# The first chunk of a fused attention and expert kernel: scores in other banks, another order of its first products, transposes done later, casts of v on another engine

## The chip, the cores and the metric

The kernel runs on one core of a Trainium2 chip. The metric is the device time of one execution in microseconds (us). The engines are named as the profile names them: PE (TensorE, the matmuls; PEld is its loading of weights), ACT (ScalarE), DVE (VectorE), POOL (GpSimd) and SP (SyncE, which issues nearly all DMAs here). Each has its own list of instructions in the program and waits for the others on semaphores.

## What is computed

For each of 8 batches, with 2496 tokens, 256 columns of v and u and 64 of z, attention without a softmax; then a choice of one of 8 experts for each token, of which an expert takes 80 at most, the ones with the largest gate.

```
scores = (z @ z.T) / S                  # z: 2496 x 64
attn   = maximum(scores, 0) ** 2
x      = u * (attn @ v)                 # v, u: 2496 x 256

expert  = argmax(x @ w_gate)            # 8 experts
for each expert e: its 80 tokens of largest gate weight
    out[token] = gate * (relu(x[token] @ w1[e]) @ w2[e])
```

Scores are symmetric in queries and keys. The kernel uses it: a block of scores is computed once, and its mirror image is gained by a transpose.

## The kernel before

Tokens are padded to 20 tiles of 128; four tiles are a chunk of queries (512 columns), so a batch (b) has five chunks (qc). Keys are taken in pairs of tiles (k, k + 1), ten pairs to a chunk; four tiles of keys are a block (j). One turn of the main loop (L1144) is a step (b, qc, r): it makes the scores of the pair that is two steps ahead (LOOK = 2) and the products of the pair of this step.

**A pair on its way.** `scores` (L396) lets PE multiply z with z, three products in a high part (zh) and a low part (zl): high by high, low by high, high by low, each for two tiles of keys that lie on the two halves of PE's rows and run together. The result s takes two PSUM banks. The pool `ps_s` has one such buffer, so PE can start a pair's scores only when ACT's Relu (L415) has emptied the buffer of the pair before. ACT then squares in place (L417), giving a, and casts it to its high part ah (L115); DVE subtracts to the low part al (L58, from L440). The casts of the first two pairs are on DVE (L117). The products (`weigh`, L452) go into acc: high v by ah, low v by ah, high v by al (the table THREE, L465); each of these, for one tile and one half of the 256 output columns, is again two matmuls that run together.

**Values.** A block of v comes by DMA into vraw, is cast to its high half (`prep_vh`, on ACT for blocks 1 to 3 of the first chunk, L1176) and its low half is subtracted on DVE (`prep_vl`, L148). Both are called vt in the rows.

**Mirrors.** In the first chunk of a batch all keys are scored. For blocks j above the chunk's own, a is also transposed on DVE (`mirror`, L312, L317), two pairs to a block, written to DRAM in a layout that completes the transpose (y, L327, two steps later), and read back (blk, L344) into one of four buffers a0 to a3 for the later chunk whose queries are block j. There `mirrored` (L377) casts and subtracts it in the place of scores. A block (i, j) in these words is the one that chunk i reads for keys of block j. A list `free` holds the buffers that no block has; a read waits until one is free, its write was issued two steps before, and its use is at most 12 steps away.

**Order.** The engines' orders are written by hand (`manual_schedule`, L1133): what stands in the code is the order on each engine. Before the loop, seven matmuls on zeros (`warm(7)`), the z blocks 0 and 1, v block 0, the scores of the first two pairs, and eight more matmuls on zeros (`warm(WARM0, True)`, L1139) in the two banks of pool `ps_m`. These matmuls on zeros are called fillers below.

Of the kernel before, what the change touches and what calls it, by code (L numbers as in the profile page):

```python
# [8 lines left out]
F32 = mybir.dt.float32  # L9
# [10 lines left out]
P = 128  # L20
# [5 lines left out]
def attn_moe_kernel(ctx, tc, zT, uT, v, wg, w1, w2, out, seq, cap):  # L26
# [114 lines left out]
    def prep_vh(b, g, raw, e0):  # L141
        vt = vpool.tile([P, QT, 2, D], F32R, tag="vt", name=f"vt_{b}_{g}")
        cp(e0, vt[:, :, 0], raw)
        v_t[b, g] = vt
# [19 lines left out]
    idle = const.tile([P, CH], BF16, name="idle")  # L164
    nc.gpsimd.memset(idle, 0.0)

    def warm(n, halves=False):
        wm = ps_m.tile([P, 2, CH], F32, tag="m", name=f"warm_{nid()}")
        for i in range(n):
            if not halves:  # L170
                nc.tensor.matmul(wm[:, 0], idle[:, :P], idle, start=True, stop=True)
                continue
            for h, hs in enumerate(HALVES):
                nc.tensor.matmul(wm[:, h], idle[hs, :P], idle[hs], start=True, stop=True)

    warm(7)
    vraw0 = load_v(0, 0)
# [124 lines left out]

    half_t, y_t, blk, slot_of, free = {}, {}, {}, {}, list(range(NA))
    n32 = P // SQ
    now, to_write = [0], []

# [65 lines left out]
    def pair_tile(tag, b, qc, k, dt=F32R, bufs=3):  # L374
        return ew.tile([P, 2, CH], dt, tag=tag, name=f"{tag}_{b}_{qc}_{k}", bufs=bufs)
# [17 lines left out]

    turned = []

    def scores(b, qc, k, turn=False):  # L396

        if k // QT < qc:
            if turn and qc % 2 == 0:
                return None, lambda: (mirrored(b, qc, k, 0), mirrored(b, qc, k, 1))  # L400
            return None, lambda: mirrored(b, qc, k)
        nq = min(CH, seq - qc * CH)
        diag = k // QT == qc and not whole_block(b, qc)
        lower = diag and k % QT > 0
        c0, c1 = (HQ, nq) if lower else (0, CH if diag else nq)
        a = pair_tile("a", b, qc, k, F32, 2)
        s = ps_s.tile([P, 2, CH], F32, tag="s", name=f"s_{b}_{qc}_{k}")
        kh, kl = (z[b, k // QT] for z in (zh_t, zl_t))
        qh, ql = (z[b, qc][:, c0:c1] for z in (zh_t, zl_t))
        for n, (zk, zq) in enumerate(((kh, qh), (kl, qh), (kh, ql))):  # L410
            for h, hs in enumerate(HALVES):
                t = k % QT + h
                nc.tensor.matmul(s[:, h, c0:c1], zk[hs, t * P:(t + 1) * P], zq[hs],  # L413
                                 start=n == 0, stop=n == 2)
        nc.scalar.activation(out=a[:, :, c0:c1], in_=s[:, :, c0:c1], func=AF.Relu)  # L415
        def square():
            nc.scalar.activation(out=a[:, :, c0:c1], in_=a[:, :, c0:c1], func=AF.Square)  # L417

        def cast():
            split(b, qc, k, a, diag, lower, c0, nq)  # L420

        if turn:
            return square, cast
        square()
        return None, cast

    def split(b, qc, k, a, diag, lower, c0, nq):
        ah = pair_tile("ah", b, qc, k)
        al = pair_tile("al", b, qc, k)
        if lower:  # L430
            m = quarter.pop((b, qc))[1].rearrange("p n k (t s) -> p k t n s", t=2)

            def natural(o):
                return o[:, :, :HQ].rearrange("p k (t n s) -> p k t n s", t=2, s=SQ)

            nc.scalar.copy(out=natural(ah), in_=m)
            tt(natural(al), m, natural(ah), ALU.subtract)
        on_v = k // QT == qc and qc == 0 or (qc, k) in ON_V and b > 0
        cp(V if on_v else nc.scalar, ah[:, :, c0:nq], a[:, :, c0:nq])
        tt(al[:, :, c0:nq], a[:, :, c0:nq], ah[:, :, c0:nq], ALU.subtract)  # L440
        if diag and not lower:
            if qc:
                quarter_out(b, qc, a)
            else:
                turned.append(lambda: quarter_out(b, qc, a))
        if k // QT > qc:
            mirror(b, k // QT, qc, k % QT, a)
        a_t[b, qc, k] = (ah, al)

# [28 lines left out]
    def attend_end(b, qc, final=()):  # L478

        k = NT - 1  # L480
        weigh(b, qc, k, 0, 0, 0, 0, False)
        weigh(b, qc, k, 0, 1, 0, 1, 0 in final)
        weigh(b, qc, k, 0, 0, 1, 0, 0 in final)
        weigh(b, qc, k, 1, 1, 1, 0, False)
        weigh(b, qc, k, 1, 0, 0, 1, 1 in final)
        weigh(b, qc, k, 1, 1, 0, 0, 1 in final)

    def attend_pair(b, qc, k, by_half=False, final=False, between=None):

# [546 lines left out]

    RAW = {(qz, 4): (2, 1)}
    WARM = 4, 3
    WARM0 = 4
    keys_in = {qc: [(qc - 1, 1, 6)] for qc in range(1, NQ)}  # L1040
    keys_in[0] = []
    keys_in[NQ - 1] = [(NQ - 2, 1, 4), (NQ - 1, 4, 7)]
# [90 lines left out]
    with tc.manual_schedule(engines={ET.PE, ET.Activation, ET.DVE, ET.SP, ET.Pool}):  # L1133
# [2 lines left out]
        prep_z(0, 1, raw12[:, 0])  # L1136
        for k in (0, 2):
            scores(0, 0, k)[1]()
        warm(WARM0, True)  # L1139
        v_raw[0, 1] = vraw1  # L1140
        z_raw.update({(0, 2): raw12[:, 1], (0, 3): raw34[:, 0], (0, 4): raw34[:, 1]})
        constants()
# [1 line left out]
        for i, (b, qc, r) in enumerate(steps):  # L1144
            last = b == B - 1 and qc == NQ - 1
            now[0] = i
            if (b, qc) == (0, 0) and r in (0, 2, 4):
                prep_z(0, r // 2 + 2, z_raw.pop((0, r // 2 + 2)))
            if i + LOOK < len(steps):
                nb, nqc, nr = steps[i + LOOK]  # L1150
                square, cast = scores(nb, nqc, 2 * pairs_of[nb, nqc][nr], r == NP - 1)
            p = pairs_of[b, qc][r]
            if r == NP - 1 and not last:
                def between(c):
                    take(b, qc, c)
                    if c == 0:
                        if square:
                            square()
                        while turned:
                            turned.pop()()  # L1160

                attend_pair(b, qc, 2 * p, True, True, between)
            if i + LOOK < len(steps):
                cast()
            shift = 1 if qc == 0 else 0
            if r == shift and prev:
                chunk_add(*prev)
            if r == 1 + shift and prev:
                chunk_x(*prev)
            if b == 0 and qc == 0:  # L1170
                if r == 5:
                    prep_vh(0, NQ - 1, v_raw[0, NQ - 1], V)
                if r % 2 == 0 and r < 8:
                    g = r // 2 + 1
                    if g < NQ - 1:
                        prep_vh(0, g, v_raw[0, g], nc.scalar)  # L1176
                    prep_vl(0, g, v_raw.pop((0, g)), V)
                    if g + 1 < NQ:
                        v_raw[0, g + 1] = load_v(0, g + 1)
                if r == 8:  # L1180
                    constants_v()
            if (b, qc, r) == (0, 2, 8):
                row_constants()
            if last and r >= NP - 2:
                if r == NP - 2:
                    for c in range(DC):
                        attend(b, qc, 2 * p, c)
            elif r < NP - 1:
                attend_pair(b, qc, 2 * p, r == 0)
            if prev:  # L1190
                finished(*prev, r)

            nb, nqc = (b, qc + 1) if qc + 1 < NQ else (b + 1, 0)
            if r == 4:
                prep_u(b, qc)
            if b + 1 < B:
                for j, load, prep in keys_in[qc]:
                    if r == prep:
                        prep_z(b + 1, j, z_raw.pop((b + 1, j)))
                    if r == load:  # L1200
                        z_raw[b + 1, j] = load_z(b + 1, j)
                if (qc, r) in V_LOAD:
                    g = V_LOAD.index((qc, r))
                    v_raw[b + 1, g] = load_v(b + 1, g)
                if (qc, r) in V_HIGH:
                    g = V_HIGH.index((qc, r))
                    prep_vh(b + 1, g, v_raw[b + 1, g], V if g == NQ - 1 else nc.scalar)
            v_low(b, qc, r)
            if qc == 0 and 0 < b < B - 1 and r < ZEROS and (b - 1) * ZEROS + r < B * NQ:
                zero_out((b - 1) * ZEROS + r, B * NQ)  # L1210
            if 2 <= b < B - 1 and qc < 2 and r in TURN:
                turn(TURN.index(r))
            if b == B - 1 and qc >= NQ - 3:
                weights_ahead(qc, r)
            if (b, qc, r) in two_at:
                two_at[b, qc, r]()
            if b == B - 1 and (qc, r) in x_at:
                x_at[qc, r]()
            mirror_back()
            mirror_out()  # L1220
            quarter_write()
            if r == 3 and not whole_block(b, qc):
                quarter_back(b, qc)
            if r == NP - 1:
                prev = b, qc
# [486 lines left out]
```

## Time and profile before

| | us |
|---|---|
| median of three runs | 1310.31 (1308.8, 1310.31, 1313.16) |
| the profiled execution, its own time | 1307.35 |
| its span, from the first to the last instruction | 1305.6 |
| PE busy in it | 1289.4 (99%) |
| DVE busy | 1062.5 (81%) |
| ACT busy | 1011.9 (78%) |

The first chunk of the first batch, with which the change deals most, lasts until about 43 us of the span. A row of the timeline has the start, the duration (of the whole group, where several instructions are merged, xN), the engine, the source line, the operation, output and inputs by their names, the shape, and in brackets the idle time of that engine before it with what ended it. Windows give the busy time of an engine in a stretch and, in brackets, how many of its instructions began there.

### The profile page before, as it was taken

The numbers are of one execution on the slowest core, as the hardware profiler recorded it, in microseconds if no ns is written. First come the engines' busy times: TensorE is split into PE (matmuls) and PEld (weight loads), VectorE is DVE, ScalarE is ACT, GpSimd is POOL, SyncE is SP. The second block draws the span as 40 slices with busy tenths as digits, with TensorE's granted clock in tenths as the row PEclk, the third lists the DMA queues.
The fourth block names the chain that finished last, engine by engine and source line by source line (L and its number), as shares of the span: only waits on it lengthen the run. The fifth ranks groups of instructions, "written<-read, shape, count | busy, mean of one in ns | idle before, by whom it ended". The sixth has DMA issues, their size and how long they took to land. (4 is left out here: it accounts for less than half of the span.)

```text
span 1305.6 us, 31273 instructions
## 1 busy us (share of the span) xinstructions
PE 1289.4 (99%) x13109; PEld 1069.3 (82%) x13109; DVE 1062.5 (81%) x1281; ACT 1011.9 (78%) x1120; POOL 53.9 (4%) x66
## 2 busy tenths in 40 slices
PE   9999999999999999999999999999999999999996
PEld 6887888888888888888888888888888888887886
DVE  8878788778886888887987788877887878877785
ACT  8877688777878678776887778876787868877785
POOL 0000000000000000001000040000000000003022
PEclk9999999999999999999999999999999999999998
DMA  6678768895989959998699967999699984789853
GB/s 209 229 233 241 218 225 261 231 267 186 277 270 261 264 202 301 262 261 257 218 308 271 283 216 231 278 265 278 221 271 257 258 254 122 237 255 257 258 189 136
DMA packets 196132, 317.21 MB, mean 243 GB/s; under 512 B 36192, under 2 KB 119056, under 8 KB 185744
## 3 DMA queue, kind: packets, MB, share of 16 engines
q1 hardware_dynamic: 194704, 312.85, 80.2%
q0 software_dynamic: 1280, 2.30, 0.6%
q8 instruction: 104, 1.70, 0.5%
q14 instruction: 44, 0.36, 0.1%
HBM read 168.77 MB, written 141.21 MB: 237 GB/s over the span
## 5 line engine op out<-in xcount | busy, mean ns | idle before, releaser
L461 PE MATMUL acc<-ah,vt 64*128 64x512 f32 (+1 forms) x6240 | 954.0, 383 | 0.7 <-ACT xf L534 0.4
L461 PEld LDWEIGHTS acc<-ah,vt 64*128 64x128 f32 x6240 | 584.7, 184 | 117.6 <-ACT xf L534 8.7
L461 PE MATMUL acc<-al,vt 64*128 64x512 f32 (+1 forms) x3120 | 610.3, 382 | 1.8 <-DVE al L58 1.5
L58 DVE TENSOR_TENSOR al<-a,ah 128x1024 fp32r<-128x1024 f32 (+1 forms) x240 | 270.7, 1128 | 139.9 <-ACT ah L115 137.5
L461 PEld LDWEIGHTS acc<-al,vt 64*128 64x128 f32 x3120 | 299.8, 184 | 59.0 <-DVE al L58 4.5
L415 ACT ACTIVATE a<-s 128x1024 f32<-128x1024 f32 x240 | 229.1, 955 | 140.4 <-PE s L413 120.1
L417 ACT ACTIVATE a<-a 128x1024 f32<-128x1024 f32 x240 | 238.1, 992 | 7.4
L58 DVE TENSOR_TENSOR al<-blk,ah 128x1024 fp32r<-128x1024 f32 (+1 forms) x176 | 194.2, 1121 | 44.9 <-ACT ah L391 44.9
L391 ACT CAST ah<-blk 128x1024 fp32r<-128x1024 f32 (+1 forms) x176 | 165.0, 973 | 74.2 <-PE acc L461 63.0
L115 ACT CAST ah<-a 128x1024 fp32r<-128x1024 f32 (+3 forms) x217 | 213.6, 984 | 5.7
L317 DVE STREAM_TRANSPOSE x<-a 128x1024 f32<-128x1024 f32 x160 | 198.1, 1238 | 0.0
L58 DVE TENSOR_TENSOR xf<-xf 128x1024 f32<-128x1024 f32 (+2 forms) x110 | 137.2, 1247 | 0.0
L413 PE MATMUL s<-zh,zl 64*128 64x512 f32 x480 | 89.7, 370 | 0.0
L413 PE MATMUL s<-zl,zh 64*128 64x512 f32 x480 | 89.6, 370 | 0.0
L534 ACT COPY xf<-acc 128x1024 f32<-128x1024 f32 x64 | 64.9, 1016 | 24.1 <-PE acc L461 24.1
L413 PE MATMUL s<-zh,zh 64*128 64x512 f32 x320 | 63.4, 393 | 0.2 <-ACT a L415 0.2
L413 PEld LDWEIGHTS s<-zl,zh 64*128 64x128 f32 x480 | 45.1, 185 | 8.2
L413 PEld LDWEIGHTS s<-zh,zl 64*128 64x128 f32 x480 | 45.2, 185 | 7.1
L148 DVE TENSOR_TENSOR vt<-vraw,vt 128x1024 fp32r<-128x1024 f32 x40 | 48.1, 1202 | 0.0
L549 DVE SCALAR_TENSOR_TENSOR xf<-xf,ut 128x1024 f32<-128x1024 f32 (+1 forms) x39 | 45.8, 1174 | 0.0
L413 PEld LDWEIGHTS s<-zh,zh 64*128 64x128 f32 x320 | 30.0, 184 | 6.6 <-ACT a L415 0.7
L634 PEld LDWEIGHTS <-xf 64*128 64x128 bf16 x1872 | 26.1, 93 | 9.9 <-issue 9.9
(203 smaller groups left out, 672.4 us busy)
## 6 DMA issues: line engine op xcount, KB each, us to landing
y<-x SPq DMA_DIRECT2D x80, 1024.0 KB
blk<-y SPq DMA_DIRECT2D x320, 256.0 KB
out<-idle SPq DMA_DIRECT2D x40, 512.0 KB
vraw<-v SPq DMA_DIRECT2D x32, 512.0 KB
ut<-uT SPq DMA_DIRECT2D x32, 512.0 KB
xu<-xf SPq DMA_DIRECT2D x32, 512.0 KB
wraw<-w SPq DMA_DIRECT2D x30, 512.0 KB
yd<-xd SPq DMA_DIRECT2D x37, 256.0 KB
```

The lines of the kernel that those rows point to most:

```text
L58: V.tensor_tensor(out=o, in0=a, in1=b, op=op)
L115: eng.copy(out=o, in_=i)
L148: e1.tensor_tensor(out=vt[:, :, 1], in0=raw, in1=vt[:, :, 0], op=ALU.subtract)
L317: V.transpose(out=x[:, :, :, t:t + 2].rearrange("p n k t s -> p t k n s"), in_=a)
L391: nc.scalar.copy(out=natural(ah), in_=src[:, rows])
L413: nc.tensor.matmul(s[:, h, c0:c1], zk[hs, t * P:(t + 1) * P], zq[hs], start=n == 0, stop=n == 2)
L415: nc.scalar.activation(out=a[:, :, c0:c1], in_=s[:, :, c0:c1], func=AF.Relu)
L417: nc.scalar.activation(out=a[:, :, c0:c1], in_=a[:, :, c0:c1], func=AF.Square)
L461: nc.tensor.matmul(acc_t[b, qc][c][:, h, :nq], v_t[b, k // QT][hs, k % QT, iv, c * P:(c + 1) * P], x[hs, k % 2, :nq], start=at not in begu ...
L534: nc.scalar.copy(out=x[:, :, c], in_=acc)
L549: V.scalar_tensor_tensor(out=x[:, 0], in0=x[:, 0], scalar=CSQ, in1=u_t[b, qc][:, :, :x.shape[-1]], op0=ALU.mult, op1=ALU.mult)
L634: nc.tensor.matmul(to[:, h, t], xb[i % 3][hs, i // 3, t0:t0 + P], wgs[hs, i // 3], start=i == 0, stop=i == 3 * DC - 1)
```

## The change

- **Banks.** The scores of the third pair of the first chunk (k = 4) go to the two banks of `ps_m` instead of `ps_s`.
- **Fillers.** The eight matmuls on zeros before the loop are left out.
- **Order of products.** In step 0 the products that need ah alone, of both tiles, come first, and those that need al after them (`attend_first`).
- **Transposes.** In the first chunk the squared scores of blocks 2, 3 and 4 are written not to the two turning buffers of a but to the buffers a1, a2 and a3, which hold them. Their six transposes are done later: both of block 2 after step 0 of chunk 1, those of block 3 after steps (1, 7) and (2, 2), those of block 4 after (2, 2) and (2, 7). The list of free buffers begins with a0 alone; a1 to a3 join when their block is transposed.
- **Casts.** The casts of v's blocks 1, 2 and 3 in the first chunk are on DVE instead of ACT.

```diff
-    def warm(n, halves=False):
+    def warm(n):
         wm = ps_m.tile([P, 2, CH], F32, tag="m", name=f"warm_{nid()}")
         for i in range(n):
-            if not halves:
-                nc.tensor.matmul(wm[:, 0], idle[:, :P], idle, start=True, stop=True)
-                continue
-            for h, hs in enumerate(HALVES):
-                nc.tensor.matmul(wm[:, h], idle[hs, :P], idle[hs], start=True, stop=True)
+            nc.tensor.matmul(wm[:, 0], idle[:, :P], idle, start=True, stop=True)
...
-    half_t, y_t, blk, slot_of, free = {}, {}, {}, {}, list(range(NA))
+    half_t, y_t, blk, slot_of, free = {}, {}, {}, {}, [0]
+    held = {}
...
+    def weights_tile(b, qc, k):
+
+        j = k // QT
+        if (b, qc) != (0, 0) or j < 2:
+            return pair_tile("a", b, qc, k, F32, 2)
+        if k % QT == 0:
+            held[j] = apool.tile([P, 2, 2, CH], F32, tag=f"a{j - 1}", name=f"a_held_{j}")
+        return held[j][:, k % QT // 2]
+
+    def mirror_held(j, t):
+        mirror(0, j, 0, t, held[j][:, t // 2])
+        if t:
+            free.append(j - 1)
+
+    held_at = {(1, 0): [(2, 0), (2, 2)], (1, 7): [(3, 0)], (2, 2): [(3, 2), (4, 0)], (2, 7): [(4, 2)]}
...
-        a = pair_tile("a", b, qc, k, F32, 2)
-        s = ps_s.tile([P, 2, CH], F32, tag="s", name=f"s_{b}_{qc}_{k}")
+        a = weights_tile(b, qc, k)
+        pool, tag = (ps_m, "m") if (b, qc, k) == (0, 0, 4) else (ps_s, "s")
+        s = pool.tile([P, 2, CH], F32, tag=tag, name=f"s_{b}_{qc}_{k}")
...
-        if k // QT > qc:
+        if k // QT > qc and ((b, qc) != (0, 0) or k // QT < 2):
             mirror(b, k // QT, qc, k % QT, a)
...
+    UPPER, LOWER = THREE[:2], THREE[2:]
+
+    def attend_first(tiles, products):
+
+        for iv, al in products:
+            for t in tiles:
+                for c in range(DC):
+                    for h in range(2):
+                        weigh(0, 0, t, c, h, iv, al, False)
...
-        warm(WARM0, True)
...
                     if g < NQ - 1:
-                        prep_vh(0, g, v_raw[0, g], nc.scalar)
+                        prep_vh(0, g, v_raw[0, g], V)
...
+            elif i == 0:
+                attend_first((0, 1), UPPER)
+                attend_first((0, 1), LOWER)
             elif r < NP - 1:
                 attend_pair(b, qc, 2 * p, r == 0)
...
+            if b == 0 and (qc, r) in held_at:
+                for j, t in held_at[qc, r]:
+                    mirror_held(j, t)
+                    if t:
+                        held.pop(j)
```

PE, from the end of the second pair's scores to the end of step 0's products, before (the numbers in a name are the chunk, the pair and a running number; x2 and x4 are matmuls in a row):

```order
L413 MATMUL s_0_2_246<-zl_0_221,zh_0_220 128x512 x2
L174 LDWEIGHTS idle
L174 MATMUL warm_259<-idle 128x512
...
L413 MATMUL s_0_4_295<-zh_0_220,zh_1_227 128x512 x2
L413 MATMUL s_0_4_295<-zh_0_220,zl_1_228 128x512 x2
L413 MATMUL s_0_4_295<-zl_0_221,zh_1_227 128x512 x2
L461 MATMUL acc_0_0_315<-ah_0_0_241,vt_0_224 128x512 x4
L461 MATMUL acc_0_0_315<-al_0_0_242,vt_0_224 128x512 x2
L461 MATMUL acc_0_0_315<-ah_0_0_241,vt_0_224 128x512 x4
L461 MATMUL acc_0_0_315<-al_0_0_242,vt_0_224 128x512 x2
L461 MATMUL acc_0_1_316<-ah_0_0_241,vt_0_224 128x512 x4
```

The same place in the changed program:

```order
L427 MATMUL s_0_2_246<-zl_0_221,zh_0_220 128x512 x2
L427 MATMUL s_0_4_286<-zh_0_220,zh_1_227 128x512 x2
L427 MATMUL s_0_4_286<-zh_0_220,zl_1_228 128x512 x2
L427 MATMUL s_0_4_286<-zl_0_221,zh_1_227 128x512 x2
L475 MATMUL acc_0_0_306<-ah_0_0_241,vt_0_224 128x512 x2
L475 MATMUL acc_0_1_307<-ah_0_0_241,vt_0_224 128x512 x2
...
L475 MATMUL acc_0_0_306<-al_0_0_242,vt_0_224 128x512 x2
L475 MATMUL acc_0_1_307<-al_0_0_242,vt_0_224 128x512 x2
L475 MATMUL acc_0_0_306<-al_0_0_242,vt_0_224 128x512 x2
L475 MATMUL acc_0_1_307<-al_0_0_242,vt_0_224 128x512 x2
L427 MATMUL s_0_6_333<-zh_0_220,zh_1_227 128x512 x2
```

The fillers are gone, the third pair's scores follow the second's, and the four groups with al now stand behind the eight with ah.

DVE in steps 0 to 3 of the first chunk, before, from the third pair's al to the second block of v and the al behind it:

```order
L58 TENSOR_TENSOR al_0_4_305<-a_0_4_294,ah_0_4_304 128x1024
L317 STREAM_TRANSPOSE x_1_0_308<-a_0_4_294 128x2x4x4x32
L148 TENSOR_TENSOR vt_1_310<-vraw_1_159,vt_1_310 128x4x256
L58 TENSOR_TENSOR al_0_6_352<-a_0_6_341,ah_0_6_351 128x1024
L317 STREAM_TRANSPOSE x_1_0_308<-a_0_6_341 128x2x4x4x32
L123 CAST zh_3_380<-raw_161 128x512
L58 TENSOR_TENSOR zl_3_381<-raw_161,zh_3_380 128x512
L58 TENSOR_TENSOR al_0_8_395<-a_0_8_384,ah_0_8_394 128x1024
L317 STREAM_TRANSPOSE x_2_0_398<-a_0_8_384 128x2x4x4x32
L148 TENSOR_TENSOR vt_2_400<-vraw_2_313,vt_2_400 128x4x256
L58 TENSOR_TENSOR al_0_10_440<-a_0_10_429,ah_0_10_439 128x1024
```

And in the changed program:

```order
L58 TENSOR_TENSOR al_0_4_296<-a_0_4_285,ah_0_4_295 128x1024
L314 STREAM_TRANSPOSE x_1_0_299<-a_0_4_285 128x2x4x4x32
L117 CAST vt_1_301<-vraw_1_159 128x4x256
L148 TENSOR_TENSOR vt_1_301<-vraw_1_159,vt_1_301 128x4x256
L58 TENSOR_TENSOR al_0_6_343<-a_0_6_332,ah_0_6_342 128x1024
L314 STREAM_TRANSPOSE x_1_0_299<-a_0_6_332 128x2x4x4x32
L123 CAST zh_3_371<-raw_161 128x512
L58 TENSOR_TENSOR zl_3_372<-raw_161,zh_3_371 128x512
L58 TENSOR_TENSOR al_0_8_386<-a_held_375,ah_0_8_385 128x1024
L117 CAST vt_2_389<-vraw_2_304 128x4x256
L148 TENSOR_TENSOR vt_2_389<-vraw_2_304,vt_2_389 128x4x256
L58 TENSOR_TENSOR al_0_10_428<-a_held_375,ah_0_10_427 128x1024
```

Block 1 keeps its transposes and gains a cast in front of the subtraction; from block 2 on, the cast stands where a transpose stood.

## Rows read from the trace of the kernel before

**Rows 1.** The page's head, its busy times by engine, and its DMA line.

```profile
span 1305.6 us, 31273 instructions
PE 1289.4 (99%) x13109; PEld 1069.3 (82%) x13109; DVE 1062.5 (81%) x1281; ACT 1011.9 (78%) x1120; POOL 53.9 (4%) x66
DMA packets 196132, 317.21 MB, mean 243 GB/s; under 512 B 36192, under 2 KB 119056, under 8 KB 185744
```

**Rows 2.** Windows: stretch, length, busy (instructions) by engine, clock, DMA share, GB/s.

```profile
10.00:20.00 10.00, 10.00 (x88) 7.89 (x87) 9.04 (x11) 9.67 (x11) 0.00 (x0) 1.00 0.18 63
50.00:60.00 10.00, 10.00 (x92) 8.27 (x90) 8.56 (x8) 9.23 (x10) 0.00 (x0) 1.00 0.64 216
```

**Rows 3.** Waits of PE, whole run: total us, times, longest.

```profile
PE acc L461 <- DVE vt L148: 0.3, 1, 0.3
```

**Rows 4.** Timeline, PE from the fillers to the first products.

```profile
1.37 3.17 PE L171 MATMUL warm<-idle 128*128 128x512 bf16 x7 [1.37 <-POOL idle L165]
...
6.93 0.50 PE L413 MATMUL s<-zh 64*128 64x512 f32 x2 [1.12 <-ACT a L415]
...
7.49 0.40 PE L413 MATMUL s<-zl,zh 64*128 64x512 f32 x2
7.73 1.04 PE L174 MATMUL warm<-idle 64*128 64x512 bf16 x8
9.01 0.50 PE L413 MATMUL s<-zh,zh 64*128 64x512 f32 x2 [0.24 <-ACT a L415]
...
9.81 0.63 PE L461 MATMUL acc<-ah,vt 64*128 64x512 f32 x4
```

**Rows 5.** Timeline, DVE and ACT from z block 1 to v block 1.

```profile
7.08 0.42 DVE L123 CAST zh<-raw 128x512 fp32r<-128x512 f32 x1
7.54 0.69 DVE L58 TENSOR_TENSOR zl<-raw,zh 128x512 fp32r<-128x512 f32 x1
...
8.15 0.69 DVE L117 CAST ah<-a 128x1024 fp32r<-128x1024 f32 x1
8.87 1.22 DVE L58 TENSOR_TENSOR al<-a,ah 128x1024 fp32r<-128x1024 f32 x1
...
12.35 1.05 ACT L115 CAST ah<-a 128x1024 fp32r<-128x1024 f32 x1
...
14.57 1.24 DVE L317 STREAM_TRANSPOSE x<-a 128x1024 f32<-128x1024 f32 x1
...
15.74 1.18 DVE L148 TENSOR_TENSOR vt<-vraw,vt 128x1024 fp32r<-128x1024 f32 x1
```

**Rows 6.** Timeline, products of steps 2, 4, 6 on PE, one row of DVE.

```profile
16.68 0.79 PE L461 MATMUL acc<-ah,vt 64*128 64x512 f32 x4
17.31 0.40 PE L461 MATMUL acc<-al,vt 64*128 64x512 f32 x2
...
23.70 0.39 PE L461 MATMUL acc<-ah,vt 64*128 64x512 f32 x2
...
24.68 0.40 PE L461 MATMUL acc<-al,vt 64*128 64x512 f32 x2
...
30.25 1.18 DVE L148 TENSOR_TENSOR vt<-vraw,vt 128x1024 fp32r<-128x1024 f32 x1
...
31.05 0.94 PE L461 MATMUL acc<-ah,vt 64*128 64x512 f32 x4
31.83 0.40 PE L461 MATMUL acc<-al,vt 64*128 64x512 f32 x2
```

**Rows 7.** Timeline of DVE, gaps in chunks 1 and 2.

```profile
50.43 1.23 DVE L58 TENSOR_TENSOR al<-a,ah 128x1024 fp32r<-128x1024 f32 x1 [1.64 <-ACT ah L115]
...
88.33 1.23 DVE L58 TENSOR_TENSOR al<-a,ah 128x1024 fp32r<-128x1024 f32 x1 [3.37 <-ACT ah L115]
```

**Rows 8.** Waits of SP's queue, whole run; timeline of ACT, chunk 3's first blocks.

```profile
SPq L344 <- DMA y<-x: 164.8, 32, 9.7
...
108.18 2.00 ACT L391 CAST ah<-blk 128x1024 fp32r<-128x1024 f32 x2
```

More of the change, by code (lines that the diff above doesn't have):

```diff
@@ L1038, in attn_moe_kernel @@
     WARM = 4, 3
-    WARM0 = 4
     keys_in = {qc: [(qc - 1, 1, 6)] for qc in range(1, NQ)}
```

## The prediction

> **What bounds the kernel now.** I began with the page's head [rows 1]: the span is 1305.6 us and PE is called busy for 1289.4 of it. That makes PE the bound almost everywhere, so an edit to another engine is worth only what it takes from, or adds to, PE's waits. Then I read the ten-us windows [rows 2]: a window in the first chunk passes 88 matmuls and the window from 50 us passes 92, both with PE "busy" for 10.00 us and the granted clock at 1.00. Busy time hides small waits here; starts must be read. The waits of PE [rows 3] show only 0.3 us for the low half of v, less than the starts give below. So I worked from the starts in the timeline.
>
> I count in slots: two matmuls on the two row halves that start together. From 24.68 to 31.05 [rows 6] PE passes 28 slots (ten left of step 4, fifteen of step 5, three of scores in step 6), so a slot is 6.37 / 28 = 0.2275 us. A step of the first chunk is three slots of scores and twelve of products.
>
> PE loses time at these places of the first chunk. Before the third pair's scores [rows 4]: the second pair's last slot starts at 7.49, fillers follow at 7.73, and the scores start only at 9.01, released by ACT's Relu, which empties the banks that they share. In steps 2, 4 and 6 [rows 6] the products wait for the low half of v: the third slot should start 0.455 after the first; it starts 0.63, 0.98 and 0.78 after it. The losses are 0.18, 0.53 and 0.33 us. All of this is about 2 us: the change aims at little, and what it can win is bounded by that.
>
> **Part by part: the start.** With other banks the third pair's scores wait for nothing of ACT. Their first slot can follow at 7.72. The second needs the low half of z block 1, which DVE ends at 7.54 + 0.69 = 8.23 [rows 5]; slots at 8.28 and 8.51, PE free at 8.74. The first products need the first pair's ah: 8.15 + 0.69 = 8.84, so about 8.9 instead of 9.81: gain **0.9 us**. The eight fillers lie in that gap and cost nothing by themselves.
>
> Upper products first: no matmul is added. The eight slots that need ah alone run from 8.9 to 10.7; al of the first pair ends at 8.87 + 1.22 = 10.09 [rows 5], in time. In the old order the third slot would stand at 9.35 and wait 0.74 for it. So this edit protects the gain, and adds none. The second pair's al follows by 0.69 + 1.22, at about 12.0, before step 1's products at about 12.4.
>
> **The casts of v.** Three casts of 1.05 (the length of ACT's cast in the row of 12.35) leave ACT and become 0.69 on DVE, the cost of the same cast in the row of 8.15 [rows 5]; from start to start 0.72 (8.15 to 8.87). They go into DVE's queue just ahead of the subtraction that makes v's low half, and that is where PE waits. In step 2 DVE cannot be earlier: pair 2's al needs an ah that ACT ends at 12.35 + 1.05 = 13.40, ACT's queue up to it is unchanged, and the transpose of 14.57 stays (it belongs to block 1). So at 15.74, where the subtraction stood, the cast now starts, and the subtraction runs from 16.46 to 17.64. PE, 0.9 early, stands at 15.8: first slot at about 16.5, second at 17.69, and the first slot after a wait takes some 0.33 (6.93 to 7.49 [rows 4] is two slots, 0.56, the second of them an ordinary one), so the third at 18.02. Before it was 17.31. PE is now **0.71 late**: the cast costs 1.6 against the early start.
>
> Bounds for this one: 0 late if the cast cost nothing (the subtraction then ends where it did), 1.05 late if it cost what ACT pays. I take 0.71, from the same operation on the same engine.
>
> **The transposes leave the first chunk.** Step 4 now starts its products at 23.70 + 0.71 = 24.41. From 17.64 DVE has al (1.22), a transpose (1.24), two z operations (0.42 + 0.69), al (1.22), the cast (0.69), all durations from [rows 5], sum 5.48: the second block's subtraction ends at 17.64 + 5.48 + 1.18 = 24.30 at the latest, before the second slot at 24.64. The old 0.53 is gone; the third slot is at 24.87 against 24.68, **0.19 late**. Step 6 starts at 31.05 + 0.19 = 31.24. Before, the low half of block 3 began at 30.25 [rows 6], behind al and a transpose; now the cast stands in the transpose's place, 0.5 shorter, so it ends near 30.9, before the second slot at 31.47. The 0.33 is gone; third slot at 31.70 against 31.83, **0.13 early**. From there ACT and DVE are both ahead of PE. Sum: -0.92 + 1.63 - 0.53 - 0.33, that is **-0.1 us**.
>
> **The six transposes in chunks 1 and 2.** Each costs 1.24 on DVE, 7.4 in all. They stand in front of operations before which DVE sat idle for ACT: two before the al at 50.43 (idle 1.64), two before the one at 88.33 (idle 3.37) [rows 7], one each at the seams of chunks 1 to 2 and 2 to 3, which have the same kind of gap. Only the first overflows, by 2.48 - 1.64 = 0.84, and PE reads that al a step of 3.4 us later. I take 0; if all cover were gone they would cost 7.4, far from any row.
>
> **Queues behind them.** The blocks (2,0), (3,0) and (4,0) are written out and read back later. The tightest is (3,0): its second transpose is the first to run in the gap before 88.33, which opens at 88.33 - 3.37 = 84.96 [rows 7], so it is done near 86.2; SP then issues the write, and a read waits for its write at most 9.7 us [rows 8], so it is issued by about 96. At the page's mean of 243 GB/s [rows 1] a block of 1 MB is an estimated 4.3 us; behind a second block, with issue, it lands by about 106. ACT takes it at 108.18 [rows 8]. I take 0.
>
> Other edits (held tiles, the list of free buffers) issue nothing.
>
> **The rivals.** (1) The lateness of step 2 is not regained, because DVE stays behind ACT or the read-back moves: +0.7 to +1.05, a median of 1311.2. For it: DVE is busy 9.04 of 10 us [rows 2]. Against: the removed transposes are longer than the added casts. (2) The cast hides better than I think, so that the early start survives: -0.9, or -1.8 with the stalls gone: 1309.0. Against it: the fixed 13.40. (3) The banks are not free early. That changes nothing in the end, since PE waits at 17.69 in any case: the same -0.1. (4) Without the fillers the clock falls. The first seven fillers, in 3.17 us [rows 4], take about 0.45 each, the lower level of 1.2 GHz; work that took 0.2275 a slot would take twice that, so a stretch as long as theirs costs about 1.6 us: 1311.9. Against it: PE is idle for 1.12 before 6.93 and the slots behind it still pass at the upper level's pace [rows 4]; the fillers' place is now filled with scores.
>
> The Trainium skill (TensorE: Matmul & The Clock Gate, section "Why this matters for your kernels") warns that idle gaps between bursts of matmuls send the array back to half rate, which speaks against dropping fillers. By that rule this would be rival 4; the traced gap of 1.12 us, longer than any that I expect between the fillers' old place and the products, left the pace up, and the sum by the rows keeps 0.
>
> (5) The slow side beyond the noise: block (3,0) lands late. Place: the seam of chunks 2 and 3. Point from which it decides: when it lands after 108.2, ACT stops, and, once PE has run through its step of about 2.4 us in hand, each further us costs one. To cost 4 us it must land near 114.6 and not by 106: 1314.3.
>
> **How the numbers follow.** The profiled execution took 1307.35 us with its span of 1305.6; the median of the runs is 1310.31, 2.96 above it. The sum gives 1307.25 there and **1310.2** for the median. Chances: forecast, with rival 3, 0.70; rival 1 0.12; rival 2 0.12; rival 4 0.04; rival 5 0.02. Mechanisms alone span 1309.0 to 1311.4; but three runs of the kernel before lie from 1308.8 to 1313.16, so a median of new runs moves by 1 to 2 us without cause. The range is therefore 1307.4 to 1312.8. A measurement of this kernel can tell about 0.3% (3.9 us) from no change. No case but rival 5 reaches that, and the whole loss of PE that the change touches is about 2 us: same 0.92, faster 0.04, slower 0.04, these two mostly from the spread of the runs.
>
> **What the new profile would show.** Right: the third pair's scores at 7.7 to 8.7 and first products near 8.9; the longest wait of PE in the first chunk in step 2, on the low half of v, until about 17.7; products of steps 4 and 6 with even slots; the first chunk ends within 0.5 us of where it did; no new PE wait at 50 to 55, 88 or 110 us. Wrong: a slot of 0.43 us after 6 us (clock), PE waiting in steps 4 or 6 again (rival 1), no wait at 17.7 (rival 2), or ACT idle for a read near 108 (rival 5).

## The result and the profile of the changed kernel

The changed kernel is slower by 0.63%: a median of 1319.37 us over 13 runs, against 1310.93 us over 13 runs of the kernel before, a ratio of 1.0063 [1.0052, 1.0073]. The forecast was no change, 1310.2 us; the time lies 6.6 us above the range. The profiled execution took 1319.07 us with a span of 1317.3. (The one of before took 1307.35, about 3.6 below the median just given, so the two traces differ by 11.7 us where the medians differ by 8.4.) All ratios here are of undisturbed executions; one of the experiment e10, of twice the time, is left out.

**Where the time went.** The page's head alone, which answers to [rows 1], shows little: PE is busy for 5 us more and the span is 12 longer.

```profile
span 1317.3 us, 31262 instructions
PE 1294.3 (98%) x13101; PEld 1072.7 (81%) x13101; DVE 1065.0 (81%) x1284; ACT 1009.9 (77%) x1117; POOL 50.6 (4%) x66
```

To find the place I compared when PE reaches the same instruction. The logits of a chunk (48 small matmuls `pl<-wgs,xf`) serve as milestones. Timeline of PE, first of before, then of after:

```profile
69.81 0.77 PE L634 MATMUL pl<-wgs,xf 64*128 64x24 bf16 x48
130.51 0.77 PE L634 MATMUL pl<-wgs,xf 64*128 64x24 bf16 x48
157.31 0.76 PE L634 MATMUL pl<-wgs,xf 64*128 64x24 bf16 x48
```

```profile
70.25 0.77 PE L658 MATMUL pl<-wgs,xf 64*128 64x24 bf16 x48
130.89 0.77 PE L658 MATMUL pl<-wgs,xf 64*128 64x24 bf16 x48
...
139.19 0.80 PE L427 MATMUL s<-zh 64*128 64x512 f32 x2 [7.54 <-ACT a L429]
...
143.85 0.40 PE L475 MATMUL acc<-al,vt 64*128 64x512 f32 x2
...
167.51 0.76 PE L658 MATMUL pl<-wgs,xf 64*128 64x24 bf16 x48
```

The changed kernel is 0.44 us behind at 70, 0.38 at 131, and 10.20 at the next milestone; so 9.82 of the loss fall in one place, the last steps of chunk 3 of the first batch. (My expectations call it the seam of chunks 3 and 4.) In after it has two parts. PE stands still for 7.54 us, waiting for ACT to empty the scores' banks. Then it runs eleven slots in 4.66 us (139.19 to 143.85), 0.42 each, where eleven of 0.2275 take 2.50: another 2.16. Together 9.7.

Why did ACT not empty them? ACT in after, timeline:

```profile
137.60 1.04 ACT L115 CAST vt<-vraw 128x1024 fp32r<-128x1024 f32 x1 [11.51 <-DMA vraw<-v]
138.55 0.59 ACT L429 ACTIVATE a<-s 128x512 f32<-128x512 f32 x1
```

ACT stood 11.51 us in front of a cast of v whose load had not landed, with the Relu that PE needs (138.55) behind it in its own queue. In before the same cast ran without a wait:

```profile
125.62 1.04 ACT L115 CAST vt<-vraw 128x1024 fp32r<-128x1024 f32 x1
```

And why was the load late? SP's queue, first of before, then of after (blk is a read of mirrored blocks, four instructions to a block; y a write of one block; yd and md the write and read of the quarter of the diagonal; vraw the loads of v):

```profile
97.99 4.56 SPq L344 DMA_DIRECT2D blk<-y  x8
...
112.51 1.73 SPq L344 DMA_DIRECT2D blk<-y  x4
114.28 0.43 SPq L361 DMA_DIRECT2D yd<-xd  x1
115.23 1.15 SPq L132 DMA_DIRECT2D vraw<-v  x2
```

```profile
87.07 0.84 SPq L324 DMA_DIRECT2D y<-x  x1
94.35 3.64 SPq L341 DMA_DIRECT2D blk<-y  x8
98.30 0.34 SPq L324 DMA_DIRECT2D y<-x  x1
109.72 2.44 SPq L341 DMA_DIRECT2D blk<-y  x4
112.26 0.85 SPq L324 DMA_DIRECT2D y<-x  x2
...
122.97 3.64 SPq L341 DMA_DIRECT2D blk<-y  x8
126.90 1.58 SPq L132 DMA_DIRECT2D vraw<-v  x2
```

In after this is a chain of turns, each a write and a read that must wait for it, and while SP stands before such a read it issues nothing else: block (3,0) is written at 87.07 and read, with (3,1), from 94.35; behind these 2 MB comes the write of (3,2) at 98.30, whose read waits until 109.72; only then the writes of (4,2) and (4,0) at 112.26; the read of (4,0) and (4,1) waits for the latter until 122.97; and the two loads of v, issued at 115.23 before, stand behind it until 126.90. The waits of SP's queue from 84 to 130 us name the writes as what ended the three waits:

```profile
SPq L341 <- DMA y<-x: 23.5, 3, 10.3
```

For a buffer to become free, the other thing that a read waits for, these reads waited 0.4 us in the same stretch. In before it is the reverse: SP stands still too, from 103.2 to 112.51, but for a buffer, and the loads of v follow that one read at 115.23. By 126.90 the transfers are the bound, as windows of after show (columns as in [rows 2]; the last two numbers are the DMA engines' share and the GB/s):

```profile
106.00:110.00 4.00, 4.00 (x38) 3.12 (x36) 3.55 (x18) 3.46 (x5) 0.00 (x0) 1.00 0.48 197
122.00:126.00 4.00, 4.00 (x40) 3.29 (x38) 4.00 (x4) 2.01 (x2) 0.00 (x0) 1.00 0.62 171
134.00:138.00 4.00, 0.00 (x0) 0.00 (x0) 0.00 (x0) 0.40 (x1) 0.00 (x0) 0.50 1.12 339
138.00:142.00 4.00, 2.81 (x14) 2.25 (x16) 1.15 (x2) 3.57 (x6) 0.00 (x0) 0.50 1.08 322
```

At the ends of the turns the DMA engines fall to about half (0.48 from 106 to 110, and 0.62 from 122 to 126). From 134 to 138 they are full while the other engines do next to nothing: the loads of v lie behind 2 MB of block reads. In before the DMA engines are busy from 122 to 126 and have slack from 134 to 138; in after it is the other way round. Windows of before:

```profile
122.00:126.00 4.00, 4.00 (x38) 3.33 (x36) 4.00 (x4) 2.39 (x3) 0.00 (x0) 1.00 1.01 308
134.00:138.00 4.00, 4.00 (x40) 3.27 (x38) 1.96 (x3) 2.64 (x4) 0.00 (x0) 1.00 0.61 213
```

### The profile page after: what moved, and what is told of

Its sections match the earlier page's. It is cut to its first block, busy times and chain, and to the rows that moved or that the text cites. A ratio compares the mean times of both kernels' runs of the same rounds, so it can differ in the third digit from the quotient of the medians.

```text
span 1317.3 us, 31262 instructions
## 1 busy us (share of the span) xinstructions
PE 1294.3 (98%) x13101; PEld 1072.7 (81%) x13101; DVE 1065.0 (81%) x1284; ACT 1009.9 (77%) x1117; POOL 50.6 (4%) x66
## 5 line engine op out<-in xcount | busy, mean ns | idle before, releaser
L58 DVE TENSOR_TENSOR al<-a,ah 128x1024 fp32r<-128x1024 f32 (+1 forms) x234 | 263.4, 1126 | 131.7 <-ACT ah L115 124.9
L429 ACT ACTIVATE a<-s 128x1024 f32<-128x1024 f32 (+1 forms) x234 | 223.1, 953 | 141.9 <-PE s L427 123.6
L431 ACT ACTIVATE a<-a 128x1024 f32<-128x1024 f32 (+1 forms) x234 | 231.7, 990 | 7.2
L115 ACT CAST ah<-a 128x1024 fp32r<-128x1024 f32 (+3 forms) x211 | 207.3, 982 | 5.5
L314 DVE STREAM_TRANSPOSE x<-a 128x1024 f32<-128x1024 f32 x154 | 190.8, 1239 | 0.0
L58 DVE TENSOR_TENSOR al<-md,ah 128x512 fp32r<-128x512 f32 x37 | 25.1, 677 | 20.4 <-PE s L427 12.2
L427 PE MATMUL s<-zh 64*128 64x512 f32 (+3 forms) x160 | 31.2, 387 | 8.7 <-ACT a L429 8.7
```

Source lines behind the costliest of these rows:

```text
L58: V.tensor_tensor(out=o, in0=a, in1=b, op=op)
L115: eng.copy(out=o, in_=i)
L314: V.transpose(out=x[:, :, :, t:t + 2].rearrange("p n k t s -> p t k n s"), in_=a)
```

## The experiments

Each was timed beside the kernel before on its chip; a ratio is to that. "Step" is what PE's milestones lose, against before, between 131 and 157 us. The expectations name their theories by letters. Q: a read that waits for a late write holds SP's queue, and the loads of v behind it. T: the DMA engines are full, whatever the order of the queue. S: the loss comes from the start, the first chunk. B (for e12 alone): half of the loss comes from reads that come bunched.

**The transposes alone (e5).** Of the change only the six late transposes are kept; fillers, banks, order of products and casts are as before.

```diff
...
+            if b == 0 and (qc, r) in held_at:
+                for j, t in held_at[qc, r]:
+                    mirror_held(j, t)
...
```

> The kernel before with one part of the change: the squared scores of blocks 2 to 4 of the first chunk are held and their six transposes done later, as in the change. Banks, fillers, order of products and casts of v are those of the kernel before. Q expects nearly the whole loss: the loads of v issued near 126 us, PE waiting 6 to 8 us near 131, ratio 1.005 to 1.008. S expects 0.999 to 1.001, since the first chunk is as before, apart from a lighter DVE.

Measured: 1.0063 [1.0050, 1.0076]. The whole loss comes with this part alone. Chunk 0 gains 1.02 us (68.79 against 69.81 at the first milestone), the step is 8.66. ACT and PE wait as in after:

```profile
134.32 1.04 ACT L115 CAST vt<-vraw 128x1024 fp32r<-128x1024 f32 x1 [9.60 <-DMA vraw<-v]
135.91 0.80 PE L430 MATMUL s<-zh 64*128 64x512 f32 x2 [5.64 <-ACT a L432]
```

**The loads of v first (e1).** The changed kernel, but the reads of (4,0) and (4,1) may not be issued ahead of the loads of v.

```diff
             b, i, j, use = to_read[0]
+            if (b, i) == (0, 4) and now[0] < 33:
+                return
```

> The changed kernel with one edit: the reads of chunk 4's blocks are held back for two steps (until step 33 of the loop), so that SP issues the two loads of the next batch's v (blocks 0 and 1) ahead of them; nothing else moves. Theory Q (queue): the write of block (4,0) is late, SP's queue stands behind it, and v's loads with it; ACT then waits for v, in order, in front of a Relu, and PE for that Relu. Q expects the loads to be issued near 115 us instead of 126.9, no wait of PE over 1 us between 100 and 160 us, no fall of the granted clock there, and a time 8 to 10 us below the changed kernel: ratio to the kernel before 0.998 to 1.002. Rival T (traffic): v lands late because the DMA engines are full, whatever the order; then ACT still waits for v by 5 us or more and the ratio stays at 1.004 or above. Rival S (start): the loss comes from the first chunk (clock, casts on DVE); then the ratio stays at 1.006.

Measured: 1.0049 [1.0033, 1.0065], a step of 8.33: Q, which looked at v alone, missed; T has the ratio (1.004 or above) but not the reason, since v was in time. The loads are now issued at 115.06 and the cast of v waits for nothing, but SP still stands in front of the block reads, and the next transfer behind them, the quarter, takes the place of v:

```profile
121.58 5.67 SPq L343 DMA_DIRECT2D blk<-y  x8
128.03 5.13 SPq L369 DMA_DIRECT2D md<-yd  x4
```

```profile
137.34 0.62 ACT L452 CAST ah<-md 128x512 fp32r<-128x512 f32 x1 [8.52 <-DMA md<-yd]
138.53 1.22 PE L477 MATMUL acc<-ah,vt 64*128 64x512 f32 x4 [4.16 <-ACT ah L115]
```

So it is not which transfer stands behind the read, but that the read stands there.

**The wait filled with matmuls on zeros (e3).** The changed kernel, with 34 fillers ahead of the logits at 130 us.

```diff
+            if i == 37:
+                warm(34)
```

> The changed kernel with 34 matmuls on zeros added on PE at the end of step 37, just ahead of the logits in front of the long wait (34 times 0.216 us is 7.3 us, about as long as the wait of 7.54 us). It tells apart what the wait costs and what the clock costs. If the clock falls because PE stands idle, it stays at full rate here, the slots after the wait last 0.23 instead of 0.43 us, and the time is about 2 us below the changed kernel: ratio to before 1.004 to 1.005. If the fall had another cause, the ratio stays at 1.006.

Measured: 1.0062 [1.0046, 1.0078]. In the trace PE goes straight on at the upper clock; the windows have 1.00 where after has 0.50:

```profile
130.20 7.51 PE L170 MATMUL warm<-idle 128*128 128x512 bf16 x34
138.69 0.41 PE L427 MATMUL s<-zh,zl 64*128 64x512 f32 x2
```

```profile
134.00:138.00 4.00, 3.94 (x37) 1.80 (x36) 0.00 (x0) 2.81 (x5) 0.00 (x0) 1.00 1.09 368
```

The step is 7.64 (here from the first milestone, since the fillers stand ahead of the second), 2.2 less than in after, which agrees with the 2.16 worked out above. The ratio does not show it (1.004 to 1.005 was expected): its interval is too wide for 2 us, and the fillers themselves last 7.51 whether or not ACT is ready.

**All transposes earlier (e2).** The changed kernel, with the second transpose of block (3,0) at the end of chunk 1 and that of (4,0) in step 2 of chunk 2.

```diff
-    held_at = {(1, 0): [(2, 0), (2, 2)], (1, 7): [(3, 0)], (2, 2): [(3, 2), (4, 0)], (2, 7): [(4, 2)]}
+    held_at = {(1, 0): [(2, 0), (2, 2)], (1, 7): [(3, 0), (3, 2)], (2, 2): [(4, 0), (4, 2)]}
```

> The changed kernel with the same six transposes placed earlier: both of block 3 after step (1, 7) and both of block 4 after step (2, 2), none after (2, 7). So block (4,0) is written some 16 us earlier and SP issues its read in chunk 2. Q expects what it expects of the run with v first: the loads of v near 115 us, no wait of PE over 1 us there, ratio 0.998 to 1.002. DVE has gaps of 2.45 and 3.37 us at these places for 2.5 us of transposes each. T expects the loss to stay, since all bytes are still moved; S expects it to stay at 1.006.

Measured: 1.0006 [0.9994, 1.0018], and no step (+0.49 to +0.50). The loads of v go out at 117.89; ACT waits 0.95 for v and PE not at all. Two table entries, moved forward by some 12 and 17 us, are the whole loss.

**One of the two at a time (e6, e12).** e6 moves only (4,0) forward, e12 only (3,0).

```diff
+    e6:  held_at = {(1, 0): [(2, 0), (2, 2)], (1, 7): [(3, 0)], (2, 2): [(3, 2), (4, 0), (4, 2)]}
+    e12: held_at = {(1, 0): [(2, 0), (2, 2)], (1, 7): [(3, 0), (3, 2)], (2, 2): [(4, 0)], (2, 7): [(4, 2)]}
```

> The changed kernel with one transpose moved: the second one of block 4 after step (2, 2) instead of (2, 7). Block 3 stays as in the change. So the write of (4,0) is issued five steps earlier, and SP meets no open write in front of chunk 4's reads, the loads of v and the quarter of chunk 3. Theory Q (the one late write holds SP's queue, and who stands behind it pays) expects the whole loss to go: no wait of PE over 1.5 us between 100 and 160 us, ratio to before 0.999 to 1.002. If the late writes of blocks 2 and 3 cost too, or the transposes on DVE (three, 3.7 us, in a gap of 3.4), the ratio is 1.003 or more.

> The changed kernel, with the second half of block (3,0) turned already in chunk 1, where its first half is, so that block (3,0) is written and read back some 12 us earlier; block (4,0) is left as late as in the changed kernel. Theory Q (only the late write of block (4,0), in front of the v loads, costs): SP stands before the read of (4,0) until about 122 as in the changed kernel, step at the seam 8 to 10 us, ratio 1.005 to 1.007. Rival B (half of the loss comes from the reads of blocks (3,0) and (4,0) that come bunched): step 3 to 6 us, ratio 1.002 to 1.004.

Measured: e6 1.0032 [1.0020, 1.0044] with a step of 4.67; e12 1.0008 [0.9994, 1.0021] with none (-0.33 to -0.34). For e6 Q had expected the whole loss to go, and missed. Both expectations for e12 missed: block (4,0) is turned as late as in after, and yet nothing is lost. SP in e12:

```profile
95.00 0.33 SPq L324 DMA_DIRECT2D y<-x  x1
101.34 2.04 SPq L341 DMA_DIRECT2D blk<-y  x4
103.48 1.02 SPq L324 DMA_DIRECT2D y<-x  x2
114.60 3.64 SPq L341 DMA_DIRECT2D blk<-y  x8
118.52 1.65 SPq L132 DMA_DIRECT2D vraw<-v  x2
```

With block (3,0) written and read earlier, the write of (3,2) at 95.00 has no 2 MB of reads in front of it, its read waits 6.3 us instead of 11.4, and the writes of (4,2) and (4,0) go out at 103.48 instead of 112.26. The read of (4,0) still waits 11 us, but from a start 9 us earlier. In after block (4,0) was turned on DVE at 103.61; what held its write until 112.26 was SP, standing in the turn before. In e6 the same turn of (3,2) is there: the write at 98.17, the read at 108.44, the loads of v at 120.99, and PE waits twice, 1.95 us for ACT and, at 159.43, 2.18 for DVE. So a late (3,0) costs half the loss alone, a late (4,0) nothing alone, and both together the whole: the turns stand one behind the other.

**When the loads of v are issued, against the loss.**

| kernel | loads of v issued, us | PE's wait for ACT there, us | step, us | ratio |
|---|---|---|---|---|
| before | 115.23 | none | 0 | 1 |
| e2 | 117.89 | none | 0.0 | 1.0006 |
| e12 | 118.52 | none | 0.0 | 1.0008 |
| e6 | 120.99 | 1.95 (and 2.18 for DVE) | 4.67 | 1.0032 |
| e5 | 123.78 | 5.64 | 8.66 | 1.0063 |
| after | 126.90 | 7.54 | 9.82 | 1.0063 |

The slack here ends somewhere between 3.3 us (e12) and 5.8 us (e6) after the time of before. Later loads cost more, though the steps are not the waits alone: in e5 and in after the fall of the clock is in them.

**SP freed, the traffic left (e10).** The changed kernel, with the reads of (4,0) and (4,1) issued from POOL's queue.

```diff
+            q = nc.gpsimd if (b, i) == (0, 4) and j < 2 else nc.sync
             for h in range(n32):
-                nc.sync.dma_start(
+                q.dma_start(
```

> The changed kernel; the reads of blocks (4,0) and (4,1) alone are issued by GpSimd's queue, so SP no longer stands in front of them. Writes, blocks, transposes and their hours stay those of the changed kernel. Theory Q (SP's queue is in order, and the read that waits for the late write of block (4,0) holds the v loads and the read of the quarter behind it): v loads issued near 115, ACT's cast of v near 126 without a wait for its load, the quarter lands before it is needed, PE's progress steps by at most 1.5 us at the seam of chunks 3 and 4, ratio 1.000 to 1.002. Rival T (the transfers of the blocks, written and read close together, fill the DMA engines, and whatever comes behind them lands late): ACT still waits over 3 us for v or for the quarter, or for block (4,0) itself, the step at the seam is 4 us or more, ratio 1.003 or more.

Measured: 1.0033 [1.0020, 1.0046]. Both theories have a part of it. As the queue's theory says, v is loaded from 115.98 and nothing is lost up to 154 us. But the loss comes back there, 8.0 us in the trace (the profiled execution took 1317.91, where the median was 1315.53). SP, POOL and ACT:

```profile
130.63 0.34 SPq L324 DMA_DIRECT2D y<-x  x1
148.54 1.74 SPq L342 DMA_DIRECT2D blk<-y  x4
```

```profile
123.88 4.75 POOL L342 DMA_DIRECT2D blk<-y  x8 [120.69 <-ACT ah L389]
156.16 1.04 ACT L389 CAST ah<-blk 128x1024 fp32r<-128x1024 f32 x1 [7.01 <-DMA blk<-y]
```

The reads still go out only at 123.88, though the row names ACT and not the write as what ended POOL's wait. The DMA engines are full from 114 to 146 us (shares of 0.98 to 1.08 in every window of 4 us), and the next turn on SP, write of (4,3) at 130.63 to its read at 148.54, now takes 17.9 us. Its late block stops ACT for 7.01. A queue of its own does not make late transfers early. The Trainium skill (DMA: Bandwidth & Descriptors, "Issuing engines are not separate DMA queues") says that DMAs of all issuing engines share the same 16 DMA engines, so that another issuer saves only the time of the sequencer to start them. The full DMA engines in e10 agree. What e10 saved besides that time is a wait: the 7 us that SP stood still in after (116.0 to 122.97).

**What the parts do to chunk 0 (e7, e8, e9, e11).** All four have the early table of e2. e7 has the fillers back, e8 the casts on ACT, e9 both; e11 is the kernel before with nothing but the transposes.

```diff
-                        prep_vh(0, g, v_raw[0, g], V)
+                        prep_vh(0, g, v_raw[0, g], nc.scalar)
...
+        warm(4, True)
```

> The changed kernel with both blocks' transposes placed early (as in the run that did that alone) and the eight fillers put back in their old place. The question is the clock at the start. If the fillers hold it, it rises near 5 us and stays, the scores and products from 7 us on pass at 0.23 a slot, and the logits of chunk 1 come 0.2 to 0.6 us earlier than in the kernel before (69.8 us). If the clock's rise has nothing to do with them, a rise near 10.4 us, or a fall after 7 us, is as likely as in the runs without fillers, and the logits come 0.5 us later than before.

> The changed kernel with both blocks' transposes placed early and the three casts of v back on ACT. By the prediction's sum, the casts on DVE cost 0.7 in step 2, later regained; without them PE waits for the low half of v until about 17.0 instead of 17.7 in step 2 and the logits of chunk 1 come some 0.9 us earlier than in the same kernel with the casts on DVE, at equal clock: about 68.9 us with the clock up from 5 us, 69.7 with a rise near 10.4. If the lateness were no matter of the casts, the third slot of step 2 would stay near 18.0.

> The changed kernel with the transposes of blocks 3 and 4 placed early, the fillers back and the casts of v on ACT; of the change remain the other banks, the order of the first products and the later transposes. Expected to be the fastest: logits of chunk 1 about 1.0 us earlier than before (68.8 us), no long wait, ratio to before 0.998 to 1.001. If the later transposes cost something beyond the one late write, 1.002 or more.

> The kernel before, with nothing of the change but the six transposes, and all of them early: two at the start of chunk 1, two at its end, two in the third step of chunk 2. Theory: taking the transposes out of chunk 0 is worth about 1.0 us there, as it was where they alone were moved, and written in time they cost nothing at the seam of chunks 3 and 4 (step at most 1.5 us): ratio 0.999 (0.998 to 1.0005). If instead any hold of these transposes costs at the seam, the step is 4 us or more and the ratio 1.003 or more.

Measured: e7 1309.48 and e8 1310.37 us in one run each beside a median of 1312.06, e9 0.9994 [0.9983, 1.0006], e11 1.0006 [0.9994, 1.0017]. None beats the kernel before by what can be measured. At the first milestone, 69.81 in before:

| | casts of v on DVE | casts of v on ACT |
|---|---|---|
| start edits, no fillers | e1, e6 -0.37; e12 -0.27; e3 -0.39; after +0.44; e2 +0.50; e10 +0.41 | e8 -1.03 |
| start edits, fillers | e7 -0.49 | e9 -0.83 |
| start as before | | e5 -1.02, e11 -0.85 |

Read across: the casts on DVE cost 0.3 to 0.7 us. Read down the right side: the start edits are worth nothing (e8 and e5 are equal). What gains is that the transposes have left chunk 0, about 1.0. In after, e2 and e10 the clock costs another 0.8 (below).

That gain does not last. Against before, e11 is 0.85 early at the first milestone and 0.90 at the one of 131 us, but 0.11 late at 157 (157.42 against 157.31); e9 and e8 go from 0.90 and 1.07 early to 0.51 and 0.77 late. So the early table has steps too, of 1.01, 1.41 and 1.84 us. In e11 PE waits there for DVE, and DVE had waited for a load of z:

```profile
151.80 0.43 DVE L123 CAST zh<-zraw 128x512 fp32r<-128x512 f32 x1 [2.95 <-DMA zraw<-zT]
155.28 0.47 PE L478 MATMUL acc<-al,vt 64*128 64x448 f32 x2 [0.74 <-DVE al L58]
```

SP issued that load at 143.76, where before did at 139.30. In both it stands behind the read of (4,3), at 140.93 against 136.46, and that read ends one more turn, from a write at 129.44 against 126.50. So, read from the trace, the same queue takes back by 157 us what chunk 0 gained, and e11, expected at 0.999, shows no ratio below 1. No run was made to keep the gain.

## Why the prediction was wrong, point by point

**The step that failed** is "Queues behind them". It took (3,0) for the tightest block, followed it to its landing, and found it in time. That much was right: the read went out at 94.35 ("by about 96"), and in after ACT takes the block at 108.57 without a wait; rival 5, which had its place there, did not come. The fault is that the step looked only at the moved block's own reader, and not at what stands behind the moved write and read in SP's queue: the write of (3,2), then the turn of (4,0), then the loads of v and the quarter, which had been on time by some 3 to 6 us (the table above). The term that it put at nothing is the delay of those loads: 11.7 us (126.90 against 115.23), which became 11.51 us of waiting on ACT and 7.54 on PE. I had the row for the longest wait of a read for its write, 9.7 us [rows 8], and used it once. Walked through the queue, it could have warned: from 86.2, three waits of 9.7 end at 115.3, and SP's issue of the reads in between (4.56 for eight, 1.73 for four, 4.56 for eight) puts the loads of v at about 126. But 9.7 is the longest of 32; with their mean, 164.8 / 32 or 5.2, the same walk ends at about 112.5, where nothing is lost. The rows of before show that the loss was possible, not that it would come. From write to read the three turns in after took 7.3, 11.4 and 10.7 us.

**Chunk 0** came out nearly as worked out, where the clock was up at its start. In e1, whose chunk 0 is that of the change:

```profile
8.84 2.11 PE L477 MATMUL acc<-ah,vt 64*128 64x512 f32 x16
16.40 0.50 PE L477 MATMUL acc<-ah,vt 64*128 64x512 f32 x2 [0.44 <-DVE vt L117]
17.66 0.50 PE L477 MATMUL acc<-ah,vt 64*128 64x512 f32 x2 [0.76 <-DVE vt L148]
17.99 0.39 PE L477 MATMUL acc<-al,vt 64*128 64x512 f32 x2
```

Forecast were 8.9, 16.5, 17.69 and 18.02; the slots of steps 4 and 6 are even as forecast, in e1 and in after; the chunk gains 0.37 where the sum said 0.13. The terms were right, then, but of a size that no median shows.

**Rival 4, the clock without the fillers,** had 0.04 and came in the profiled execution of after. PE at the start of after, to be held against [rows 4]:

```profile
7.84 0.63 PE L427 MATMUL s<-zh,zl 64*128 64x512 f32 x2
8.27 0.63 PE L427 MATMUL s<-zl,zh 64*128 64x512 f32 x2
9.97 2.23 PE L475 MATMUL acc<-ah,vt 64*128 64x512 f32 x16
18.45 0.50 PE L475 MATMUL acc<-ah,vt 64*128 64x512 f32 x2 [0.76 <-DVE vt L148]
```

Slots of 0.43 until 9.97 are the sign that the prediction named (a slot of 0.43 us after 6 us) and the lower level of 1.2 GHz; before had 0.23 a slot there. It is the pace that tells: the clock column of the windows has 1.00 from 7 to 10 us in both kernels, as it has from 0 to 5, where the seven fillers take 0.45 each. The first products come at 9.97 instead of 8.84, and chunk 0 ends 0.42 us later than in before (43.87 against 43.45). The forecast price of 1.6 was too high: part of it goes into the wait of step 2, and 0.8 is left (+0.44 in after against -0.37 in e1). My reason against it, that the pace stayed up through a gap of 1.12 us, did not hold: in after the pace was at the lower level before the gap already (5.07 to 5.50 is 0.43). What differs there is when the clock rose, not that it fell in the gap.

**The six transposes on DVE** cost nothing, as taken: PE is 0.42 behind at the end of chunk 0 and 0.38 at the logits of 131. The al that [rows 7] has at 50.43 came at 51.41, 0.98 later, of which 0.44 is the start.

**Rival 1 and rival 2** did not decide; **rival 3** was not met, since the third pair's scores follow directly (7.58 in e1).

**What stays open.** About 1.5 us of the 11.7 between the two traces lie later than 200 us (PE is 10.19 behind at 200 us, and the span is 11.7 longer); no run was made for them. And whether the 0.8 us of the clock enter the median was not settled: of the kernels without the eight fillers, four of eight profiled executions had slots at the lower level after 8 us (after, e2, e10, and e3 at no cost), of the five with them none. That is suggestive, no proof.

## What to carry to other kernels

When work is moved later, follow its write and its read through the queue that issues them, and write down what stands behind each and when that is needed; the block's own reader may be the least of the cost. A read that must wait for a write in a queue that issues everything else is a turn of 6 to 11 us here, most of it a stretch in which nothing else starts, and several turns add up. A table of due times is cheap to shift: two entries moved forward took the whole loss away. And a gain early on counts only if the loads further down can follow: 0.9 us won by 131 us in e11 were gone at 157.

## What the runs showed of the hardware

- **The clock falls in a wait and is paid for after it.** After PE's 7.54 us without a matmul the granted clock was 0.50 from 134 to 142 us (in e1, after a wait of 4.16, from 138 to 142), and eleven slots cost 2.16 us extra; with fillers in the same wait (e3) it stayed at 1.00. In e6, with waits of 1.95 and 2.18, it stayed up. The Trainium skill (TensorE: Matmul & The Clock Gate, "Why this matters for your kernels") warns of idle gaps between bursts of matmuls; these rows agree.
- **At the start the clock rises at different times in kernels whose first 5 us are the same.** Seven fillers in 3.17 us stand at the head of each; slots of 0.23 stand from 7.12 on in e1 and only after 9.97 in after. In e3 they slow down again: the windows give 0.65 from 7 to 9 us and 0.67 from 9 to 12.
- **A turn from write to read was longer where more was in flight.** The read of (3,2) was issued 6.3 us after its write in e12, 11.4 in after with 2 MB of reads ahead of the write, and the one of (4,3) 17.9 us after in e10 with the DMA engines full. These rows go together; no run changed the traffic alone.
